# Folding the attention output of eight sets in one group of 256-column matmuls

## Chip, cores, metric

One core of a Trainium2 chip. The metric is the device time of one execution in microseconds (us); the profile's span leaves out some 1.8 us of it (196.2 us of 198.0 here). Engines: PE does matmuls, DVE and ACT work on vectors, SP issues the loads. In the profile's lines `bank` is PSUM, the memory that PE writes its results to, and `slots` are the buffers in on-chip memory that the loads fill. DMA engines (the page counts 16) move the bytes of the loads; in the trace a load lands in increments of a counter, its semaphore.

## The reference

One decode step of a gated mix: grouped-query attention over the last 4096 positions of a KV cache (4 sequences, 32 query heads, 8 KV heads, head size 128), projected by `wo`, mixed by a sigmoid gate with a gated ReLU FFN of the same input. All inputs are bf16.

```python
g = _sigmoid((x * gate_w).sum(-1, keepdims=True))      # x: 4 x 1 x 512
# A: q = x @ wq; softmax(q k^T / sqrt(128)) v over 4096 cached positions; o @ wo  (4096 x 512)
# B: h = relu-gated (x @ W_gate) * (x @ W_up); h @ W_down  (1792 x 512)
return g * A + (1 - g) * B
```

Nearly all the work is reading: 33.6 MB of K, 33.6 MB of V and 13.9 MB of weights.

## The kernel before

K and V are worked through in eight "sets" of 4 MB (one sequence, four KV heads). For each set: DVE transposes K, PE computes scores, ACT takes the exponential, DVE transposes it, PE multiplies by V (`PV`), and ACT copies the 128 x 512 result to `osb` (`NORM`). A "fold" (`OQ`) then picks the right rows and columns of `osb` with 0/1 matrices and sums them into the layout that the output projection (`WO`) needs; DVE evicts it (copies it out of PSUM), times the softmax and gate factors, into `oq`. The kernel before folds twice, after sets 0 to 3 (early) and after sets 4 to 7 (at the end). Other names in the code: `KT` and `PT` are the transposes of K and of the exponential, `SC` the scores, `SW` spreads the row maximum, `RS` sums the softmax denominators, `GU` is the gate and up products of B, `FFN` its down product.

```python
WO_PIECES = ((0, 8), (8, 16), (16, 24), (24, 28), (28, 30), (30, 31), (31, 32))
LOW4 = (0, 124, 128)                                   # rows of the last piece: 124, then 4

# order of the program (shortened)
for s in range(1, NSET):
    o += [("KT", s, 0), ("SC", s - 1, 3)] + [("RS", 0), ("OQ", 0)] * (s == 5) + [("SW", s - 1)]
    # ... cut ...
o += [("SC", s, 3), ("SW", s), ("PV", s - 1), ("PT", s), ("RS", 1), ("GU",), ("PV", s), ("FFN",), ("OQ", 1)]
return o + [("WO", p) for p in range(len(WO_PIECES))]

# order of the loads, all from one queue
o = [("wq",), ("x",), ("gw",), ("k", 0), ("k", 1), ("v", 0)]
for s in range(2, NSET):
    o += [("k", s), ("v", s - 1)]
return o + [("wg",), ("wu",), ("v", NSET - 1), ("wd",)] + [("wo", p) for p in range(len(WO_PIECES))]

def OQ(g):                                             # PE, 16 matmuls of 128 columns
    key = ("OQ", g)
    r = 64 * g
    for t in range(2):
        for cc in range(2):
            for c in range(4):
                x = 256 * t + 128 * cc + 32 * c
                first, lastmm = (t, cc, c) == (0, 0, 0), (t, cc, c) == (1, 1, 3)
                mm(banks[tr(key)][r:r + 64, 0:128], R["fold"][:, 2 * cc + t, c, :], osb[:, :, x:x + 32], first,
                   lastmm, ev=key if lastmm else None, pos=(0, r),
                   waits=tr_free(key) + [("NORM", 4 * g + 3), ("FOLD", 7)] if first else ())

def EOQ(g):                                            # DVE, 64 x 128 out of PSUM
    # ... cut: oq[64 g : 64 g + 64] = bank * recip ...

def NORM(s):                                           # ACT
    E.op(lambda: a.activation(osb[:, s % 4, :], ob(s), ACTF.Copy), ev=("NORM", s),
         waits=[("PV", s)] + ([("OQ", 0)] if s >= 4 else []))

def WO(p):                                             # PE, 2 matmuls per row block, 64 in all
    w = [("WO", p, n) for n in range(len(wo_rows(p)))] + [("E", "OQ", g) for g in range(2)]
    # ... cut: a group of matmuls waits for its piece of Wo and for both folds ...
```

## Time and profile before

| | before |
|---|---|
| time, median of 6 runs of the comparison | 198.05 us (197.97 to 198.31) |
| span of the profiled run | 196.2 us |
| read from HBM | 81.01 MB |
| PE busy, DVE busy | 124.0 us, 124.3 us |

The head of the page of the kernel before: the span, and two of its strips of 40 slices (4.9 us each). DMA is the busy share of the 16 DMA engines in tenths, GB/s what they moved.

```profile
span 196.2 us, 1783 instructions
...
DMA  6999999999999999999999999999999999999990
GB/s 220 434 429 434 441 434 454 441 431 428 434 428 434 429 428 424 428 428 428 428 428 428 424 434 428 441 428 428 428 444 428 441 400 456 434 404 413 423 370 28
```

The DMA engines are busy from the second slice to the last but one, while PE and DVE are busy for 63% of the span. Most slices lie at 424 to 441 GB/s, single ones at 454 and 456, and the mean of the 37 slices from the second to the third last is 430 (413 over the whole span).

The end of the chain of waits of the kernel before (start us, us, what), with one K load from the middle of it:

```profile
125.67 24.73 DMA slots<-in_A_k_cache_dram
...
174.07 19.42 DMA slots<-in_A_wo_dram
...
193.62 0.29 PE bank L326 x2
...
193.94 0.42 DVE osum L582
```

The K load lands 24.7 us after DVE's work let it be issued. A 4 MB set takes about 10 us at this rate (an estimate, 4.19 MB over 430 GB/s), so the queue holds some 15 us of work ahead of it (an estimate, 24.7 less 10). At the end the chain takes up the last Wo load at its issue at 174.07 us and waits for it until 193.5; after it only two matmuls, a 0.42 us copy and the store are left.

The tail of the timeline of the kernel before (start us, duration, engine, line, operation, tiles, shapes, count; in brackets the engine's idle time just before and what ended it). Lines of other engines and of weight loads are cut.

```profile
178.56 6.11 PE L326 MATMUL bank<-slots,pT 128*64 128x512 bf16 x32 [5.73 <-DMA slots<-in_A_v_cache_dram]
...
184.61 1.69 PE L326 MATMUL bank<-slots,hg 128*4 128x256 bf16 x28
184.72 0.60 ACT L608 ACTIVATE osb<-bank 128x512 bf16<-128x512 f32 x1 [12.04 <-PE bank L326]
...
186.23 1.08 PE L326 MATMUL bank<-osb,fold 128*64 128x128 bf16 x16
187.35 0.45 DVE L561 TENSOR_TENSOR oq<-bank,recip 64x128 bf16<-64x128 f32 x1 [12.51 <-PE bank L326]
...
187.94 1.91 PE L326 MATMUL bank<-slots,oq 128*4 128x256 bf16 x32 [0.63 <-DVE oq L561]
...
190.22 1.04 PE L326 MATMUL bank<-slots,oq 128*4 128x256 bf16 x16 [0.36 <-DMA slots<-in_A_wo_dram]
...
191.47 0.60 PE L326 MATMUL bank<-slots,oq 128*4 128x256 bf16 x8 [0.22 <-DMA slots<-in_A_wo_dram]
...
192.28 0.68 PE L326 MATMUL bank<-slots,oq 128*4 128x256 bf16 x6 [0.21 <-DMA slots<-in_A_wo_dram]
...
193.62 0.27 PE L326 MATMUL bank<-slots,oq 128*4 128x256 bf16 x2 [0.66 <-DMA slots<-in_A_wo_dram]
193.94 0.42 DVE L582 CAST osum<-bank 128x256 bf16<-128x256 f32 x1 [6.14 <-PE bank L326]
```

This is the stretch that the change touches. The last PV product ends at 184.6, the FFN's product follows, then the fold (16 matmuls in 1.08 us), its eviction (0.45 us) and Wo. The first 32 Wo matmuls run back to back; ahead of all later ones PE waits for Wo data. The waits of PE in that stretch (what waited, for what: us in total, times, longest):

```profile
PE bank L326 <- DMA slots<-in_A_wo_dram: 1.5, 4, 0.7
PE bank L326 <- DVE oq L561: 0.6, 1, 0.6
```

### The profile page before, as it was taken

To read this page: it belongs to the slowest core of one execution; us is meant where nothing else is said; L and a number is where in the kernel's file an instruction comes from. 1 tells how busy PE (TensorE), PEld (TensorE's weight loads), DVE (VectorE), ACT (ScalarE), POOL (GpSimd) and SP (SyncE) were. 2 spreads that over 40 slices of the span, in tenths; PEclk is the share of its full clock that TensorE was granted. 3 is DMA by queue.
4 is the path that set the end of the run, shared out by engine and by line. 5 is a ranking of instruction groups with operands and counts; after the bars stand their busy time and mean duration, and the time that the engine had idled before them with its cause. 6 is when DMAs were issued, how large, how long until landed. Compare 5 with 4: busy or idle time off the path is not lost.

```text
span 196.2 us, 1783 instructions
## 1 busy us (share of the span) xinstructions
PE 124.0 (63%) x741; PEld 52.5 (27%) x741; DVE 124.3 (63%) x153; ACT 27.3 (14%) x33; POOL 9.6 (5%) x25
## 2 busy tenths in 40 slices
PE   0419267573974797389439755956694646925973
PEld 0214122121421242133114411412241212403551
DVE  6103688999579838982996299739963997440000
ACT  2213000040031004001400140014001400510100
POOL 7830000000000000000000000000000000000000
PEclk9999859997899579969999978995899699995799
DMA  6999999999999999999999999999999999999990
GB/s 220 434 429 434 441 434 454 441 431 428 434 428 434 429 428 424 428 428 428 428 428 428 424 434 428 441 428 428 428 444 428 441 400 456 434 404 413 423 370 28
DMA packets 4055, 81.12 MB, mean 413 GB/s; under 512 B 580, under 2 KB 848, under 8 KB 1104
## 3 DMA queue, kind: packets, MB, share of 16 engines
q1 hardware_dynamic: 4040, 81.01, 96.8%
q8 instruction: 6, 0.10, 0.2%
q14 instruction: 1, 0.01, 0.0%
q10 hardware_dynamic: 8, 0.00, 0.0%
HBM read 81.01 MB, written 0.00 MB: 413 GB/s over the span
## 4 chain that ended last, share of the span: by engine, by line
DMA 41%; DVE 31%; PE 19%; issue 6%; SPq 2%; ACT 0%
DMA slots<-in_A_k_cache_dram 25%; DVE kt L498 21%; PE bank L326 17%; DMA slots<-in_A_wo_dram 10%; DMA gwT<-in_gate_w_dram 6%; DVE sc L534 5%; SPq L261 2%; PE bank L330 2%; DVE qblk L524 1%; DVE pT L549 1%; DVE rd L538 1%; DVE negmax L544 0%; ACT gwB L604 0%; DVE oq L561 0%; DVE osum L582 0%
## 5 line engine op out<-in xcount | busy, mean ns | idle before, releaser
L326 PE MATMUL bank<-kt,qblk 128*128 128x512 bf16 x256 | 71.8, 431 | 29.8 <-DVE kt L498 29.8
L498 DVE STREAM_TRANSPOSE kt<-slots 128x2048 f32<-128x2048 f32 x32 | 73.7, 2305 | 24.4 <-DMA slots<-in_A_k_cache_dram 24.4
L326 PEld LDWEIGHTS bank<-kt,qblk 128*128 128x128 bf16 x256 | 25.0, 107 | 71.4 <-DVE kt L498 37.8
L326 PE MATMUL bank<-slots,pT 128*64 128x512 bf16 x256 | 33.4, 420 | 5.7 <-DMA slots<-in_A_v_cache_dram 5.7
L534 DVE CUSTOM_DVE_ANT_0 sc<-bank,maskf 128x512 bf16<-128x512 f32 x32 | 21.1, 661 | 5.9 <-PE bank L326 5.9
L623 ACT ACTIVATE pe<-sc,negmax 128x2048 bf16<-128x2048 bf16 x8 | 16.0, 2002 | 58.9 <-DVE negmax L544 58.9
L326 PEld LDWEIGHTS bank<-slots,pT 128*64 128x64 bf16 x256 | 15.5, 121 | 23.9 <-issue 14.5
L549 DVE STREAM_TRANSPOSE pT<-pe 128x2048 bf16<-128x2048 bf16 x8 | 18.5, 2312 | 2.2 <-ACT pe L623 2.2
L608 ACT ACTIVATE osb<-bank 128x512 bf16<-128x512 f32 x8 | 4.8, 597 | 83.8 <-PE bank L326 83.8
L326 PE MATMUL bank<-rd,grpb 128*128 128x32 bf16 x8 | 1.6, 194 | 18.8 <-DVE rd L538 15.4
L561 DVE TENSOR_TENSOR oq<-bank,recip 64x128 bf16<-64x128 f32 x2 | 0.9, 441 | 12.6 <-PE bank L326 12.5
L326 PEld LDWEIGHTS bank<-rd,grpb 128*128 128x128 bf16 x8 | 0.8, 98 | 22.4 <-DVE rd L538 18.9
L326 PE MATMUL bank<-slots,oq 128*4 128x256 bf16 x64 | 4.5, 272 | 2.1 <-DMA slots<-in_A_wo_dram 1.5
L326 PE MATMUL bank<-slots,xT 128*4 128x512 bf16 (+1 forms) x64 | 5.3, 490 | 0.0
L502 DVE COPY xT<-bank 128x16 bf16<-128x16 bf16 x1 | 0.2, 167 | 8.0 <-PE bank L330 8.0
L524 DVE TENSOR_SCALAR qblk<-bank 32x64 uint32<-32x64 uint32 x16 | 2.9, 215 | 3.3 <-PE bank L330 3.2
L326 PE MATMUL bank<-maskr,maskl 128*128 128x512 bf16 x1 | 0.6, 608 | 5.9 <-POOL maskr L302 5.9
L582 DVE CAST osum<-bank 128x256 bf16<-128x256 f32 x1 | 0.4, 424 | 6.1 <-PE bank L326 6.1
L326 PEld LDWEIGHTS bank<-slots,oq 128*4 128x4 bf16 x64 | 2.6, 83 | 4.0 <-DMA slots<-in_A_wo_dram 2.8
L330 PE MATMUL bank<-identb,xsb 4*128 4x4 bf16 x4 | 0.3, 166 | 5.2 <-DMA xsb<-in_A_x_dram 5.2
L302 POOL TENSOR_SCALAR_AFFINE_SELECT fold<-fold 128x256 bf16<-128x256 bf16 x8 | 3.4, 419 | 1.1
L493 DVE MEMSET qblk<- 128x2304 uint32 x1 | 2.0, 1978 | 1.4 <-PEq L646 1.4
(58 smaller groups left out, 43.8 us busy)
## 6 DMA issues: line engine op xcount, KB each, us to landing
slots<-in_A_k_cache_dram SPq DMA_DIRECT2D x8, 4096.0 KB, 24.8
slots<-in_A_v_cache_dram SPq DMA_DIRECT2D x8, 4096.0 KB, 30.6
slots<-in_A_wq_dram SPq DMA_DIRECT2D x1, 4096.0 KB, 12.4
slots<-in_A_wo_dram SPq DMA_DIRECT2D x3, 1024.0 KB, 16.4
slots<-in_B_W_gate_dram SPq DMA_DIRECT2D x1, 1792.0 KB, 19.7
slots<-in_B_W_up_dram SPq DMA_DIRECT2D x1, 1792.0 KB, 23.6
slots<-in_B_W_down_dram SPq DMA_DIRECT2D x1, 1792.0 KB, 18.5
slots<-in_A_wo_dram SPq DMA_DIRECT2D x1, 512.0 KB, 19.2
```

The source lines that it names most:

```text
L261: E.op(lambda: e.dma_start(dst, src), ev=ev, waits=waits, ctr=ctr)
L302: op(lambda: e.affine_select(dst, src, pattern, cmp, fill, base=base, channel_multiplier=mult), ev)
L326: E.op(lambda: t.matmul(out_, lhsT, rhs, start=start, stop=stop, tile_position=pos, skip_group_check=True), ev=ev, waits=waits)
L330: E.op(lambda: t.transpose(out_, in_, idn), ev=ev, waits=waits)
L493: E.op(lambda: v.memset(qblk[:, :, :, :, :].rearrange("p s h c e -> p (s h c e)"), 0.0), ev=("QZ",))
L498: E.op(lambda: v.transpose(kt[:, f, :].bitcast(FP32), slot("k", s)[:, 4096 * f:4096 * f + 4096].bitcast(FP32)), ev=("E", "KT", s, f), waits=w)
L524: E.op(lambda dst=dst, r=r, g=g: v.tensor_scalar(dst, src[r, g, 0:B, :, :], 0, None, op0=ALU.bitwise_or), ev=("E",) + keys[1] if (q, g) == ...
L534: E.op(lambda: v.tensor_tensor_reduce(sc[:, 512 * f:512 * f + 512], banks[scb(key)], R["maskf"][:, :], 1.0, -3.0e38, ALU.add, ALU.max, mx4 ...
L538: E.op(lambda: v.tensor_tensor(rd32[:, :, :], bc(R["own8"][:, :].unsqueeze(2), 2, 4), bc(mx4[:, :].unsqueeze(1), 1, 8), ALU.mult), ev=("MA ...
L549: E.op(lambda: v.transpose(pT[:, s % 2, :], pe[:, :]), ev=("E", "PT", s), waits=[("EXP", s)] + ([("PV", s - 2)] if s >= 2 else []))
L608: E.op(lambda: a.activation(osb[:, s % 4, :], ob(s), ACTF.Copy), ev=("NORM", s), waits=[("PV", s)] + ([("OQ", 0)] if s >= 4 else []))
L623: E.op(lambda: a.activation(pe[:, :], sc[:, :], ACTF.Exp, bias=negmax[:, s % 2:s % 2 + 1], scale=SCALE, accum_out=rowsum[:, s:s + 1]), ev= ...
```

## The change

Intent: do the fold once, for all eight sets, with matmuls twice as wide, so that the early fold and its waits vanish from the middle of the kernel; keep the eight results in `osb` until then; and make the constant tables bf16. The last 128 KB of Wo stay in two loads of 124 and 4 rows. The diff's core (buffer declarations and renamed waits cut):

```diff
-    sb("osb", [128, 4, 512], BF16)
+    sb("osb", [128, NSET, 512], BF16)
-    sb("ee", [16, 128], FP32)
-    sb("e4", [16, 128], FP32)
+    sb("ee", [16, 128], BF16)
+    sb("e4", [16, 128], BF16)
@@ order
-        o += [...] + [("RS", 0), ("OQ", 0)] * (s == 5) + [("SW", s - 1)]
+        o += [...] + [("RS", 0)] * (s == 5) + [("SW", s - 1)]
@@ PE
-                        mm(banks[tr(key)][r:r + 64, 0:128], R["fold"][:, 2 * cc + t, c, :], osb[:, :, x:x + 32], first,
-                           lastmm, ev=key if lastmm else None, pos=(0, r),
-                           waits=tr_free(key) + [("NORM", 4 * g + 3), ("FOLD", 7)] if first else ())
+                        mm(banks[tr(key)][0:64, 0:256], R["fold"][:, 2 * cc + t, c, :], osb[:, :, x:x + 32], first, lastmm,
+                           ev=key if lastmm else None, pos=(0, 0),
+                           waits=tr_free(key) + [("NORM", NSET - 1), ("FOLD", 7)] if first else ())
@@ DVE: two evictions at the end, the second from partitions 0-63 to 64-127
+            for g in range(2):
+                r = slice(64 * g, 64 * g + 64)
+                E.op(lambda g=g, r=r: v.tensor_tensor(oq[r, :, :]..., banks[tr(key)][0:64, 128 * g:128 * g + 128]..., ...
@@ ACT
-            E.op(lambda: a.activation(osb[:, s % 4, :], ob(s), ACTF.Copy), ev=("NORM", s),
-                 waits=[("PV", s)] + ([("OQ", 0)] if s >= 4 else []))
+            E.op(lambda: a.activation(osb[:, s, :], ob(s), ACTF.Copy), ev=("NORM", s),
+                 waits=[("PV", s)])
```

More of the change, by code (lines that the diff above doesn't have):

```diff
@@ L137, in _alloc @@
     sb("rowsum", [128, NSET], FP32)
-    sb("recip", [128, 2, 4], FP32)
+    sb("recip", [128, 4, 4], FP32)
     sb("ge", [128, 2, 4], FP32)
@@ L151, in _order @@
     for s in range(1, NSET):
-        o += [("KT", s, 0), ("SC", s - 1, 3)] + [("RS", 0), ("OQ", 0)] * (s == 5) + [("SW", s - 1)]
+        o += [("KT", s, 0), ("SC", s - 1, 3)] + [("RS", 0)] * (s == 5) + [("SW", s - 1)]
         o += [("KT", s, 1), ("PT", s - 1), ("SC", s, 0), ("KT", s, 2), ("SC", s, 1), ("KT", s, 3)]
@@ L155, in _order @@
     s = NSET - 1
-    o += [("SC", s, 3), ("SW", s), ("PV", s - 1), ("PT", s), ("RS", 1), ("GU",), ("PV", s), ("FFN",), ("OQ", 1)]
+    o += [("SC", s, 3), ("SW", s), ("PV", s - 1), ("PT", s), ("RS", 1), ("GU",), ("PV", s), ("FFN",), ("OQ",)]
     return o + [("WO", p) for p in range(len(WO_PIECES))]
@@ L399, in PV, with OQ @@
                        (f, c) in ((3, 12), (3, 14)), ev=("PV", s) if (f, c) == (3, 14) else None, waits=w, pos=(0, r))
-        def OQ(g):
-            key = ("OQ", g)
-            r = 64 * g
+        def OQ():
+            key = ("OQ",)
             for t in range(2):
@@ L432, in WO @@
             lo, hi = WO_PIECES[p]
-            w = [("WO", p, n) for n in range(len(wo_rows(p)))] + [("E", "OQ", g) for g in range(2)]
+            w = [("WO", p, n) for n in range(len(wo_rows(p)))] + [("E", "OQ")]
             for i in range(lo, hi):
@@ L476, in _program @@
         elif k == "OQ":
-            dve.append(("EOQ", it[1]))
+            dve.append(("EOQ",))
     dve.append(("FIN",))
@@ L553, in ERS, with EOQ @@
             key = ("RS", g)
-            E.op(lambda: v.reciprocal(recip[:, 0, :], banks[tr(key)][:, 0:4]), ev=("E",) + key, waits=[key])
-            E.op(lambda: v.tensor_tensor(recip[:, 1, :], recip[:, 0, :], gg[:, 0, :], ALU.mult), ev=("RG", g),
+            E.op(lambda: v.reciprocal(recip[:, 2 * g, :], banks[tr(key)][:, 0:4]), ev=("E",) + key, waits=[key])
+            E.op(lambda: v.tensor_tensor(recip[:, 2 * g + 1, :], recip[:, 2 * g, :], gg[:, 0, :], ALU.mult), ev=("RG", g),
                  waits=[("E",) + key, ("G",)])
-        def EOQ(g):
-            key = ("OQ", g)
-            r = slice(64 * g, 64 * g + 64)
-            E.op(lambda: v.tensor_tensor(oq[r, :, :].rearrange("p i b -> p b i"),
-                                         banks[tr(key)][r, 0:128].rearrange("p (b i) -> p b i", b=4),
-                                         bc(recip[r, 1, :].unsqueeze(2), 2, 32), ALU.mult), ev=("E",) + key,
-                 waits=[key, ("RG", g)])
+        def EOQ():
+            key = ("OQ",)
+            for g in range(2):
+                r = slice(64 * g, 64 * g + 64)
+                E.op(lambda g=g, r=r: v.tensor_tensor(
+                    oq[r, :, :].rearrange("p i b -> p b i"),
+                    banks[tr(key)][0:64, 128 * g:128 * g + 128].rearrange("p (b i) -> p b i", b=4),
+                    bc(recip[0:64, 2 * g + 1, :].unsqueeze(2), 2, 32), ALU.mult), ev=("E",) + key if g else None,
+                    waits=[key, ("RG", 1)])
         def H():
```

## The prediction

> **What bounds the kernel now.** The load stream. The page's strip of 40 slices shows the DMA engines at 90% or more in all slices but the first and last, at about 430 GB/s. [...] In the chain of waits, K loads land 24.8 us after their issue; a 4 MB load at 430 GB/s takes about 9.8 us (my estimate), so some 15 us of work is queued ahead: freeing a slot a little earlier or later changes nothing. At the end the chain goes from the issue of the last Wo load (174.1 us) 19.4 us to its landing at 193.5, then two matmuls, a 0.42 us copy and the store. In the timeline PE waits for Wo data ahead of every piece after the first two (starts at 190.2, 191.5, 192.3, 192.7, 193.6 us).
>
> **What changes, costed from the timeline.**
> 1. Around 110 us the first fold goes: 16 matmuls, 1.08 us of PE, and one 0.44 us DVE eviction. K slots come free 0.4 us sooner, but the queue has backlog. Worth nothing.
> 2. Near the end, sixteen 128-column matmuls (186.2 to 187.3 us, 67 ns each) become sixteen of 256 columns. The 512-column score matmuls at the full clock run 8 in 1.91 us, 239 ns each with the drain; half is 0.12 us. [...] My estimate for the group is 1.8 to 1.9 us: +0.75 us.
> 3. One 0.45 us eviction before Wo becomes two in a row: +0.4 us. The first Wo matmul starts at about 189.1 instead of 187.9.
> 4. bf16 fold constants: two products of 0.79 us each at 6.5 to 8 us get shorter. PE then idles until x lands at 13.2 us. Worth nothing.
> 5. The attention copies' wait on the first fold goes; they were not late. The Wo pieces and the 124 + 4 rows stay.
>
> **How much is critical.** The 1.15 us delay sits in PE's Wo backlog. Before, the first 32 Wo matmuls took 1.91 us (60 ns each), then PE waited for data. After: 32 by 191.0, the third piece by 191.95, the fourth by 192.5, the fifth by 192.75, the sixth by 192.9. The last piece lands at 193.5 as before; PE has caught up with 0.6 us to spare. Nothing of the change reaches the end.
>
> **Prediction: 198.1 us**, range 197.6 to 198.8. Faster by over 2%: 0.01; within 2%: 0.975; slower by over 2%: 0.015.
>
> **What would show the steps right or wrong.** The DMA strip and the landing of the last Wo load unchanged; one fold group of 16 matmuls of 128x256, 1.8 to 1.9 us, after the last attention copy; two evictions of about 0.44 us; first Wo matmul about 1.1 us later; PE's waits for Wo data nearly gone for the third to fifth piece, but one of about 0.6 us still there before the last two matmuls; the final copy starting within 0.2 us of 193.9.
>
> **What would make it wrong.** If the PE clock were throttled in the last 7 us (it is at 0.50 from about 177 to 183, after an idle stretch of PE), the fold would take about 3.5 us and Wo twice as long: some 3 us late, 1.5% slower. If fold matmuls cost much more than 0.12 us, or the evictions that cross partitions much more than 0.45 us, the 0.6 us of slack would be used up and the excess would show in full. If the last Wo bytes landed sooner, PE's backlog would hide the gain.

Item 2 came to 1.8 to 1.9 us for the group, +0.75 us; half of 239 ns gives 16 x 0.12 = 1.9 us by itself, +0.8 us. The sum: 0.75 + 0.4 = 1.15 us later, none of it past the last landing, so 198.1 us.

## The result, and the profile after

| | before | after |
|---|---|---|
| time, median of 6 runs each | 198.05 us (197.97 to 198.31) | 197.99 us (197.68 to 198.09) |
| span of the profiled run | 196.2 us | 196.2 us |
| PE busy, matmul instructions | 124.0 us, 741 | 121.8 us, 723 |
| DVE busy | 124.3 us | 124.1 us |

The ratio is 0.9991, 95% interval 0.9978 to 1.0003: the same. Here and below a ratio is the mean time of one kernel's runs over that of the other's of the same rounds, so it is not quite the ratio of the medians quoted.

The same strips of the page, after:

```profile
span 196.2 us, 1747 instructions
...
DMA  6999999999999999999999999999999999989990
GB/s 234 441 429 428 428 474 434 424 434 434 428 434 429 421 424 428 428 428 428 428 428 428 424 434 428 434 434 434 434 441 438 434 389 466 454 386 407 418 365 25
```

The same parts of the chain of waits, after:

```profile
125.29 25.05 DMA slots<-in_A_k_cache_dram
...
174.00 19.50 DMA slots<-in_A_wo_dram
...
193.63 0.29 PE bank L326 x2
...
193.95 0.42 DVE osum L583
```

In this pair of executions the end of the stream is the same to within 0.1 us: last issue at 174.0 instead of 174.07, last landing at 193.5, final copy at 193.95 instead of 193.94. (Over the eight profiles with all bytes and the 124 + 4 rows, the last landing lies at 193.43 to 193.69 us, so so close a match is partly luck.) The K load in the middle shows why time saved there is lost: it is issued 0.38 us sooner than before (125.29 instead of 125.67) and lands 0.06 us sooner (150.34 instead of 150.40). The tail of the timeline after:

```profile
178.63 6.26 PE L326 MATMUL bank<-slots,pT 128*64 128x512 bf16 x32 [5.86 <-DMA slots<-in_A_v_cache_dram]
...
184.82 1.69 PE L326 MATMUL bank<-slots,hg 128*4 128x256 bf16 x28
184.93 0.60 ACT L609 ACTIVATE osb<-bank 128x512 bf16<-128x512 f32 x1 [12.32 <-PE bank L326]
...
186.45 1.94 PE L326 MATMUL bank<-osb,fold 128*64 128x256 bf16 x16
188.42 0.88 DVE L561 TENSOR_TENSOR oq<-bank,recip 64x128 bf16<-64x128 f32 x2 [13.65 <-PE bank L326]
...
189.45 3.59 PE L326 MATMUL bank<-slots,oq 128*4 128x256 bf16 x62 [1.06 <-DVE oq L561]
...
193.63 0.27 PE L326 MATMUL bank<-slots,oq 128*4 128x256 bf16 x2 [0.60 <-DMA slots<-in_A_wo_dram]
193.95 0.42 DVE L583 CAST osum<-bank 128x256 bf16<-128x256 f32 x1 [4.65 <-PE bank L326]
```

One fold group of 16 matmuls of 128x256 takes 1.94 us where the late group of before took 1.08; two evictions take 0.88 us; Wo starts at 189.45 instead of 187.94, 1.5 us later (0.2 us of that because the last PV product ended later). Then 62 Wo matmuls run back to back, without the waits of before, and the last two wait 0.60 us for the last bytes as they did before (0.66 us). PE's waits in this stretch, after:

```profile
PE bank L326 <- DVE oq L561: 1.1, 1, 1.1
PE bank L326 <- DMA slots<-in_A_wo_dram: 0.6, 1, 0.6
```

So the waiting for Wo data shrank from 1.5 to 0.6 us, and the longer wait for the fold took its place: 0.6 before, 1.1 after. PE's late cost was paid out of time in which it would have waited for data.

### The profile page after: what moved, and what is told of

Same layout as the page of the kernel before. It is cut to its first block, busy times and chain, and to the rows that moved or that the text cites. A ratio compares the mean times of both kernels' runs of the same rounds, so it can differ in the third digit from the quotient of the medians.

```text
span 196.2 us, 1747 instructions
## 1 busy us (share of the span) xinstructions
PE 121.8 (62%) x723; PEld 50.9 (26%) x723; DVE 124.1 (63%) x153; ACT 27.2 (14%) x33; POOL 9.5 (5%) x25
## 4 chain that ended last, share of the span: by engine, by line
DMA 58%; DVE 29%; PE 5%; issue 4%; SPq 2%
DMA slots<-in_A_k_cache_dram 48%; DVE kt L497 21%; DMA slots<-in_A_wo_dram 10%; PE bank L326 5%; DVE sc L533 5%; SPq L261 2%; DVE pT L548 1%; DVE rd L537 1%; DVE negmax L543 0%; DVE osum L583 0%; DVE mx L533 0%; DVE recip L554 0%; DVE recip L553 0%
## 5 line engine op out<-in xcount | busy, mean ns | idle before, releaser
L326 PE MATMUL bank<-kt,qblk 128*128 128x512 bf16 x256 | 73.0, 436 | 27.8 <-DVE kt L497 27.8
L326 PE MATMUL bank<-slots,oq 128*4 128x256 bf16 x64 | 3.9, 272 | 1.7 <-DVE oq L561 1.1
L326 PE MATMUL bank<-slots,xT 128*4 128x512 bf16 (+1 forms) x64 | 4.8, 460 | 0.0
```

Of the source, the lines that this page charges most:

```text
L326: E.op(lambda: t.matmul(out_, lhsT, rhs, start=start, stop=stop, tile_position=pos, skip_group_check=True), ev=ev, waits=waits)
```

## Experiments

Main theory: the stream of loads sets the time; the early saving and the bf16 tables are worth nothing, since loads are queued far ahead, and the late cost fits in PE's slack ahead of the last Wo bytes. Rival 1: the early saving is real and just pays for a real late cost. Rival 2: the late chain is not near the path at all, so its slack was not touched. A third question came up on the way: what sets the size of the slack. Each run below was timed against the kernel before on the same chip, in 5 rounds; differences in us are of mean times. None was timed against the changed kernel in the same rounds. That kernel lay 0.18 us under the kernel before in its own comparison (95% interval -0.44 to +0.06), so a difference from the changed kernel is known only to some 0.35 us (an estimate from the two intervals). What each run does is told below the table. "(before)" marks an experiment on the kernel before, all others are on the changed one.

| run | median (lowest to highest), us | mean difference, us | ratio, 95% interval |
|---|---|---|---|
| a_fold20 | 198.14 (197.78 to 198.48) | +0.13 | 1.0006, 0.9994 to 1.0018 |
| a_fold32 | 198.80 (198.08 to 199.33) | +0.77 | 1.0038, 1.0019 to 1.0057 |
| b_fold48 (before) | 198.07 (197.89 to 198.74) | +0.18 | 1.0008, 0.9994 to 1.0022 |
| a_one128 | 197.38 (197.25 to 197.50) | -0.59 | 0.9969, 0.9957 to 0.9981 |
| b_wdhalf (before) | 196.11 (195.86 to 196.37) | -1.97 | 0.9902, 0.9889 to 0.9914 |
| a_wdhalf | 196.63 (196.09 to 197.18) | -1.40 | 0.9930, 0.9914 to 0.9946 |
| a_early | 198.06 (197.80 to 198.15) | -0.07 | 0.9998, 0.9986 to 1.0010 |
| b_one128 (before) | 197.20 (197.12 to 197.43) | -0.83 | 0.9960, 0.9947 to 0.9972 |
| a_wuhalf | 195.99 (195.83 to 196.12) | -2.20 | 0.9889, 0.9875 to 0.9902 |
| a_fp32c | 198.10 (197.75 to 198.38) | -0.07 | 0.9996, 0.9983 to 1.0009 |
| a_warm_fold32 | 197.96 (197.76 to 198.16) | -0.10 | 0.9995, 0.9981 to 1.0009 |
| a_warm_one128 | 197.24 (197.17 to 197.75) | -0.76 | 0.9961, 0.9948 to 0.9975 |

### More fold work: how much fits in the slack

Three runs put extra fold matmuls ahead of the late group; the group then overwrites their result.

```diff
+            for n in range(4):        # a_fold20; 16 for a_fold32
+                mm(banks[tr(key)][0:64, 0:256], R["fold"][:, 0, n % 4, :], osb[:, :, 32 * (n % 4):32 * (n % 4) + 32], True, True, ...)
             for t in range(2):        # the group as it was
```

> The changed kernel with 4 more fold matmuls of 256 columns ahead of the group (20 instead of 16, result unchanged). Main theory: the tail waits for the last Wo bytes and PE is done 0.6 us before them, so +0.45 us of fold (4 x 0.11 us) changes nothing: 198.0 us, within 0.1 us; the wait before the last two matmuls shrinks from 0.60 to about 0.15 us. Rival (fold work is on the path, and the late cost was paid back by the early saving): +0.45 us.

The time stayed (+0.13 us, the interval holds 1). In the profile the group of 20 took 2.37 us instead of 1.94 for 16, 0.11 us per matmul, and PE still waited 0.61 us ahead of the last two matmuls; the wait did not shrink since the last PV product had ended 0.8 us sooner in this execution. That part of the expectation missed, and it pointed to something that varies (below).

> The changed kernel with 16 more fold matmuls of 256 columns (32 instead of 16, result unchanged): +1.8 us of PE work. Main theory: 0.6 us of it is absorbed, the rest shows: +1.0 to +1.2 us, about 199.1 us, and no wait for Wo data is left before the last two matmuls. Rival (fold work is on the path in full): +1.8 us. Rival (fold work is never on the path): 0.

The timeline of that run's profile, its fold, evictions, Wo and final copy:

```profile
186.89 3.68 PE L326 MATMUL bank<-osb,fold 128*64 128x256 bf16 x32
190.61 0.88 DVE L564 TENSOR_TENSOR oq<-bank,recip 64x128 bf16<-64x128 f32 x2 [15.45 <-PE bank L326]
...
191.64 3.66 PE L326 MATMUL bank<-slots,oq 128*4 128x256 bf16 x64 [1.07 <-DVE oq L564]
195.34 0.42 DVE L586 CAST osum<-bank 128x256 bf16<-128x256 f32 x1 [3.85 <-PE bank L326]
```

The fold takes 3.68 us, no wait is left within the 64 Wo matmuls, and the final copy starts at 195.34 instead of 193.95. So the chain of the fold does reach the end once it is long enough: Rival 2 is out. The mean rose by 0.77 us, less than the 1.0 to 1.2 expected, and the six runs scatter over 1.25 us (198.08 to 199.33), two and a half times the range of the kernel before on the same chip (0.50). Sixteen matmuls more made the group 1.74 us longer, 109 ns each (3.68 less 1.94 us, over 16).

In the kernel before, 32 more of its 128-column matmuls were put into the late group:

```diff
+                for n in range(32 * g):   # b_fold48
+                    mm(banks[tr(key)][r:r + 64, 0:128], R["fold"][:, 0, n % 4, :], osb[...], True, True, ...)
```

> The kernel before with 32 more fold matmuls of 128 columns in its late group (48 instead of 16, result unchanged): +1.9 us of PE work, about as much as in the run with 32 of 256 columns. Main theory: the kernel before had about 2.1 us of slack there (0.6 us plus the 1.5 us by which the first Wo matmul moved), so 0 to +0.1 us. Rival (on the path in full): +1.9 us.

The group took 2.87 us instead of 1.08, and the time stayed within the interval (+0.18 us; five runs at 197.9 to 198.13 and one at 198.74). The same extra length that costs the changed kernel 0.77 us fits into the slack of the kernel before (the two intervals overlap a little, 1.0019 to 1.0022). That is what the change used up.

### The early fold put back, the tables put back

```diff
+    ("OQD",) after ("RS", 0) at s == 5     # a_early: 16 fold matmuls of 128 columns and one eviction,
+                                           # into rows of oq that are overwritten at the end
```

> The changed kernel with the early fold put back as dummy work: 16 fold matmuls of 128 columns and one eviction after the fourth set, whose result is overwritten at the end (result unchanged). Main theory: there PE and DVE wait for loads that have 15 us of queue ahead of them, so 1.1 us of PE and 0.44 us of DVE more change nothing: 0, within 0.1 us. Rival (the change is worth nothing because an early saving paid for the late cost): +0.4 us (the DVE part) to +1.5 us.

No change. In its profile the dummy group took 1.08 us of PE at 112 us and its eviction 0.44 us of DVE at 115 us, as long as in the kernel before. By Rival 1 this kernel, with the early work and the late cost, is 0.4 us or more slower than the kernel before; the interval (0.9986 to 1.0010, at most +0.20 us) excludes it. Against the changed kernel the difference is about +0.1 us, give or take 0.35, which excludes most of what Rival 1 expected but not its lowest value. The landing of the K load above, which barely moved, speaks against it too. The wait of the copies (`NORM`) on the early fold was not put back.

```diff
-    sb("ee", [16, 128], BF16)              # a_fp32c
+    sb("ee", [16, 128], FP32)              # and e4 the same
```

> The changed kernel with the two constant tables back in fp32 (result unchanged). Main theory: the two products at 6.5 to 8 us get about 0.3 us or more longer each, and PE then idles until x lands at 13 us: 0, within 0.1 us. Rival (the head is on the path): up to +0.8 us.

No change, though the products are dear in fp32: 0.79 us each, with two matmul records per product, against 0.28 us each, with one, in bf16 (profile of the change). After them PE idles until x lands, at 13.3 us in this profile and 13.1 in that of the change.

### Fewer bytes, before and behind the last V load

```diff
-    load(("WD",), "d_wd", Wd, ...)
+    load(("WD",), "d_wd", Wd[:, 0:3584], ...[:, 0:3584])     # b_wdhalf, a_wdhalf
-    load(("WU",), "d_wu", Wu, ...)
+    load(("WU",), "d_wu", Wu[:, 0:3584], ...[:, 0:3584])     # a_wuhalf
```

All three give a wrong result (half of a weight is stale data); the instructions stay.

> The changed kernel with half of W_up not loaded (wrong result on purpose): 0.92 MB less ahead of the last V load instead of behind it, matmuls as they are. Main theory: the stream sets the time, and here the last PV product, the fold and Wo all move up with it, so the full 2.1 us shows: -1.9 to -2.2 us, about 195.9 us, with the last V load landing at about 176.4 us instead of 178.6. Rival (PE or DVE sets the time): much less.

-2.20 us, the full length of the missing stream: 0.92 MB in 2.20 us is 417 GB/s. The stream sets the time.

> The kernel before with half of Wd not loaded (the other half of its columns is computed from stale data: wrong result on purpose). 0.92 MB less behind the last V load, 2.1 us of stream at 430 GB/s; the matmuls stay. Main theory: the stream's end sets the time and PE has about 2.1 us of slack behind it, so nearly all shows: -1.9 to -2.1 us, about 196.0 us. Rival (PE's fold and Wo chain is already on the path): less than -0.7 us.

-1.97 us: the kernel before follows the stream nearly all the way. (In its profile, the slowest of the four runs, PE was the last: the last Wo bytes landed at 191.64 us and the final copy started at 192.39.)

> The changed kernel with the same half of Wd not loaded (wrong result on purpose). Main theory: the change used up 1.5 us of PE's slack; the Wo bytes land at about 191.4 us but PE can't finish its 64 Wo matmuls before about 193.2 us (62 of them ended at 193.04 in the profile of the change), so only -0.7 us shows, up to -1.2 in runs in which the last PV product meets a faster clock: about 197.0 to 197.3 us. Rival (the change left the slack as it was): as much as for the kernel before, -1.9 to -2.1 us.

-1.40 us. The changed kernel can't follow: 0.57 us of the gain is lost to PE (the two intervals just touch, at 0.9914). The direction is that of the main theory, the size is off, as the expectation allowed at most -1.2 us. The profiles say why. The start of the FFN's product and of the final copy, in the changed kernel with half of Wd:

```profile
184.32 1.69 PE L326 MATMUL bank<-slots,hg 128*4 128x256 bf16 x28
...
192.64 0.42 DVE L583 CAST osum<-bank 128x256 bf16<-128x256 f32 x1 [3.85 <-PE bank L326]
```

and in the kernel before with half of Wd:

```profile
185.35 1.69 PE L326 MATMUL bank<-slots,hg 128*4 128x256 bf16 x28
...
192.39 0.42 DVE L582 CAST osum<-bank 128x256 bf16<-128x256 f32 x1 [3.85 <-PE bank L326]
```

In both, Wo ran without a wait for data. From the FFN's start to the final copy the changed kernel needs 8.32 us, the kernel before 7.04: the change made this chain 1.28 us longer (0.86 us of fold, 0.43 of eviction). But the chain's start differs by 1.03 us between the two profiles, the other way round. So the cost of the change is fixed, and the slack that it is taken from is not.

### What sets the slack

The start of the chain is the end of the last PV product. Granted clock (PEclk) in the changed kernel's profile, in stretches of 2 us:

```profile
core 0: us, PE busy (x) PEld busy (x) DVE busy (x) ACT busy (x) POOL busy (x), PEclk, DMA share, GB/s
176.00:178.00 2.00, 0.00 (x0) 0.00 (x0) 0.00 (x0) 0.00 (x0) 0.00 (x0) 0.79 0.94 397
...
180.00:182.00 2.00, 2.00 (x12) 0.93 (x10) 0.00 (x0) 0.00 (x0) 0.00 (x0) 0.50 0.96 401
182.00:184.00 2.00, 2.00 (x12) 1.05 (x10) 0.00 (x0) 0.00 (x0) 0.00 (x0) 0.51 0.99 410
184.00:186.00 2.00, 2.00 (x30) 1.22 (x28) 0.00 (x0) 0.60 (x1) 0.00 (x0) 1.00 1.01 418
```

PE has nothing to do from 173 to 178.6 us, and the clock falls to 0.50; the last PV product then takes 6.26 us, against 3.64 us at the full clock (a_wuhalf). After waits for V of 5.1 us or more (5.10 in b_one128, 5.86 in the changed kernel) the slow spell came, after 3.1 us (a_wuhalf) it did not. In the clock records of the profiles before and after the change, all changes of the clock lie whole multiples of 3.413 us apart, and the spell starts at 176.78 us in one and 177.15 in the other, though PE began to wait at much the same time (172.8). From the trace's clock records, each row one profiled execution:

```
run            slow spell, us     last PV product, us      FFN starts, us
a_fold20       178.5 to 182.0     178.95 to 184.06         183.99
b_one128       175.7 to 182.6     178.53 to 184.15         184.08
a_wdhalf       175.7 to 182.5     179.05 to 184.39         184.32
before         176.8 to 183.6     178.56 to 184.67         184.61
a_fp32c        176.7 to 183.5     178.69 to 184.68         184.61
b_fold48       177.2 to 184.0     178.46 to 184.81         184.74
after          177.2 to 184.0     178.63 to 184.89         184.82
a_one128       177.3 to 184.1     178.99 to 185.16         185.09
a_early        177.8 to 184.6     178.69 to 185.26         185.19
a_fold32       177.9 to 184.8     178.74 to 185.34         185.27
b_wdhalf       178.0 to 184.8     178.86 to 185.42         185.35
a_wuhalf       none               176.63 to 180.27         180.92
```

The spell starts anywhere from 175.7 to 178.5 us and lasts 3.4 or 6.8 us, so the chain starts anywhere from 184.0 to 185.35 us. The slack ahead of the last bytes moves with it, by up to 1.4 us: from 0.60 us at a start of 184.82, an estimate gives 0.1 to 1.4 us. Sixteen more matmuls (1.74 us) would then cost 0.3 to 1.7 us; the six runs of a_fold32 lay 0.1 to 1.4 us above the mean of the kernel before. This is the candidate for its scatter.

How busy PE was ahead of the changes was counted in the same two profiles, in stretches of 3.413 us that begin and end at such multiples (PE's busy share as the profile models it). PE was busy for 0 to 37% of each of the 17 stretches after which the clock fell from 1.00 to 0.50, and for 40% or more of the 63 after which it stayed at 1.00; for 79% or more of the 17 after which it came back, and for 4 to 77% of the 6 after which it stayed at 0.50. These are counts of two executions, not limits of the hardware.

To test whether the spell sets the slack, PE was kept busy in that stretch (in a_warm_fold32 together with the 32 fold matmuls, in a_warm_one128 below with the last Wo rows in one load):

```diff
+            for n in range(20):       # after the gate and up products, ahead of the last PV product
+                mm(banks[tr(("OQ",))], identb[:, :], R["maskr"][:, :], True, True, ...)   # overwritten by the fold
```

> The changed kernel with 32 instead of 16 late fold matmuls, and with 20 dummy matmuls of 512 columns (0.22 us each, about 4.4 us) in PE's idle stretch ahead of the last PV product (result unchanged). With 32 fold matmuls alone the time rose by 0.75 us on average and scattered from 0 to 1.3 us; in the profiles the last PV product took 5.3 to 6.6 us with the clock at 0.50, and 3.64 us at the full clock in the run with half of W_up, where PE had idled only 3.1 us before it. Theory: the slack is set by where that slow clock falls. With PE kept busy the product takes 3.6 to 4 us, the chain gains 2 us or more, and the same 1.8 us of extra fold is hidden again: 198.0 us within 0.15 us, with a small scatter. Rival (the extra fold costs time by itself, whatever the clock): +0.75 us, or more if the dummies only add work.

The granted clock, and lines of the timeline, of a_warm_fold32:

```profile
176.00:178.00 2.00, 1.39 (x7) 0.42 (x5) 0.00 (x0) 0.00 (x0) 0.00 (x0) 1.00 0.89 376
178.00:180.00 2.00, 1.29 (x12) 0.87 (x14) 0.00 (x0) 0.00 (x0) 0.00 (x0) 1.00 0.96 409
180.00:182.00 2.00, 2.00 (x22) 1.27 (x18) 0.00 (x0) 0.00 (x0) 0.00 (x0) 1.00 1.01 424
```

```profile
173.13 4.26 PE L326 MATMUL bank<-maskr,identb 128*128 128x512 bf16 x19 [0.16 <-issue]
...
178.71 3.64 PE L326 MATMUL bank<-slots,pT 128*64 128x512 bf16 x32 [1.32 <-DMA slots<-in_A_v_cache_dram]
...
184.64 3.68 PE L326 MATMUL bank<-osb,fold 128*64 128x256 bf16 x32
...
193.56 0.28 PE L326 MATMUL bank<-slots,oq 128*4 128x256 bf16 x2 [0.33 <-DMA slots<-in_A_wo_dram]
```

The slow spell is gone, the PV product takes 3.64 us, and 32 fold matmuls, the same 3.68 us as in a_fold32, now cost nothing (-0.10 us; the five runs within 0.4 us). So the slow clock sets the slack: without it the same extra work fits. That single timed runs of a_fold32 scatter by the spell's position fits this but was not seen run by run, since only one execution of each kernel was profiled.

### The last 128 KB

The stream thins out in its last microseconds. Here is the GB/s strip of the changed kernel from 190 to 194 us, 0.1 us per slice:

```profile
GB/s 307 348 461 195 328 297 102 246 266 174 184 225 225 195 164 195 164 113 72 72 61 41 20 20 31 20 20 31 10 0 0 0 0 0 0 0 0 0 0 0
```

The slices at about 20 GB/s at the end are a single stream of packets: in the packet records the last 15 packets of 1 KB start one after another from 192.24 to 192.84 us, 42 ns apart, which is 24 GB/s. The completion records say which load it is (increments of the semaphore of each of the last three loads, in us; the last two have one more record each, 0.17 us after the end of their issue):

```
128 rows (last but two): ten at 190.69 to 191.06, then 192.07 192.46 192.50 192.54 192.71 192.72
124 rows:                (one at 174.12) 192.16 192.21 192.49 193.31
4 rows:                  (one at 183.78) 192.34 192.39 192.67 193.50
```

So 124 and 4 rows land in four increments each, where the 128 rows of the load before had 16. In equal shares four would have 31 packets of 1 KB each, 1.3 us at 42 ns, and 16 would have eight, 0.3 us (estimates from the rows, the increments and the 42 ns). One of the four comes about a microsecond after the other three (193.31 against 192.16 to 192.49), as six of the 16 of the load before came after its ten (192.07 to 192.72 against 190.69 to 191.06). The issue of the 4 rows itself took 9.6 us (174.0 to 183.6; the seven Wo issues before it 0.33 to 0.44); no record says why, and as it ended ten us ahead of the landing, nothing shows that it cost time here.

```diff
-LOW4 = (0, 124, 128)
+LOW4 = (0, 128)                       # a_one128, b_one128
```

> The changed kernel with the last 128 KB loaded in one piece of 128 rows instead of 124 and 4. The trace shows four completion increments for each of the two last loads, at 192.3, 192.4, 192.7 and 193.5 us, and sixteen for the loads before, of which ten come about a microsecond before the last six (the last at 192.7). [...]: -0.4 us in time, all of it seen since PE is ready at 193.04. If the split was right for this tail, the landing stays at 193.5 or comes later: 0 or more.

The same strip in a_one128:

```profile
GB/s 318 420 410 369 389 379 184 256 143 184 184 143 143 143 133 113 123 102 133 133 92 92 51 41 20 20 31 0 0 0 0 0 0 0 0 0 0 0 0 0
```

The last load lands at 193.15 us, and the time falls by 0.59 us against the kernel before, clear of zero; against the changed kernel it is about 0.4, as expected, give or take 0.35 (in the profile the final copy starts 0.45 us sooner; one execution).

> The kernel before with the last 128 KB in one piece of 128 rows. In the changed kernel this gave -0.6 us, with the last load landing at 193.15 us and the last two Wo matmuls starting at 193.19. Main theory: the gain is the load's own and does not need the change: -0.4 to -0.6 us here too, the last load landing at about 193.1 to 193.2 us. Rival (the gain needs the changed fold): 0.

-0.83 us in the kernel before, so the gain is the load's own; its last load landed at 192.84 us. It is no smaller without the changed fold.

> The changed kernel with the same 20 dummy matmuls and the last 128 KB in one piece of 128 rows (result unchanged). The last load lands at about 192.9 to 193.2 us as in the two runs of that piece, and PE is ready more than 2 us before it. Theory: at least the -0.6 us that the piece gave in the changed kernel, up to the -0.8 us that it gave in the kernel before: 197.2 to 197.4 us, with PE waiting for data ahead of the last pieces. Rival (PE still ties with the load in this tail): -0.6 us and no wait left. If the dummies cost something of their own, the gain is less.

-0.76 us, and in the profile PE's weight loads wait for data ahead of the last five groups of Wo matmuls. So the changed kernel seems to get the full gain once PE has its slack back. The intervals of the three runs overlap (0.9957 to 0.9981, 0.9947 to 0.9972, 0.9948 to 0.9975), so the 0.2 us between a_one128 and the other two is not settled.

The edit changes two things at once: the number of increments in which the last bytes land (four for each of the two loads; the load of 128 rows above had 16) and the number of loads (one instead of two). No run separates them. The landings give a reading: with 124 + 4 rows the last bytes landed at 193.57 us on average (eight profiles), with 128 at 192.96 (three), 0.6 us sooner. In each of the eight, the 4 rows landed about 0.2 us after the 124, so about a third of the gain may belong to the second load and the rest to the fewer increments (an estimate, 0.2 of 0.6 us).

b_one128 and a_warm_one128 are the fastest correct kernels here, 0.4% under the kernel before, b_one128 with one line changed.

## Why the prediction was right

It said 198.1 us, within 197.6 to 198.8; 197.99 was measured.

- The stream bounds the kernel: shown. 0.92 MB less of it took 2.20 us off (a_wuhalf), and the last landing did not move (193.49 and 193.50, in a spread of 193.43 to 193.69 over the profiles).
- The early fold and the bf16 tables are worth nothing: putting each back left the time where it was (a_early, a_fp32c: both -0.07 us against the kernel before, intervals around 1). A saving of up to some 0.4 us against the changed kernel is not excluded by the times alone; the K load, issued 0.38 us sooner and landed 0.06 us sooner, shows the mechanism.
- The late fold costs 1.8 to 1.9 us in place of 1.08: 1.94 measured, +0.86 instead of +0.75 us. The evictions: 0.88 us for two, 0.43 more. The first Wo matmul at 189.45, where 189.1 was predicted; 0.2 us of the difference is the later end of the PV product.
- PE catches up with 0.6 us to spare: 0.60 us in the profile. That is one execution, and so close a match is partly luck: with the early work put back the profile showed 0.43. The slack depends on where the slow clock falls, and the prediction treated it as one number; it did name the slow spell as the risk, though it placed it in the last 7 us, and the profiles have it end by 184.8 us.
- Only one remark failed: that PE's backlog would hide the gain of earlier Wo bytes. It hides at most a part of it: a_one128 was 0.59 us faster than the kernel before, where b_one128 was 0.83 faster.

The change is thus no faster and no slower, but not free: it lengthened PE's last chain by 1.28 us. With half of Wd gone, the kernel before was 1.97 us faster than with all of it, and the changed one 1.40 us faster than that same kernel.

## What to carry to other kernels

Here loads bound the kernel and were queued some 15 us ahead, so compute saved in the middle was worth nothing (putting it back: -0.07 us against the kernel before), and compute added at the end was free only up to the slack ahead of the last bytes (+0.13 us for four more fold matmuls, +0.77 for sixteen). In a kernel of this kind, measure that slack by adding dummy work until the time moves. Read it from more than one execution: here PE's clock fell to 0.50 after PE had waited 5.1 us or more, from 175.7 to 178.5 us in different executions, and the start of its last chain moved by 1.4 us. Dummy matmuls in that stretch made room for 1.74 us of extra work after it (-0.10 us). And look at the last loads by themselves: one load of 128 rows in place of 124 and 4 was worth more here (0.59 and 0.83 us under the kernel before) than the whole change (0.18).
